# Windowed attention and a gated MLP on one core: all four first scores ahead of the first product, another order of decoding, and a stored 1e-9

## The chip, the core and the metric

The kernel runs on one core of a Trainium2 chip. A core has a matrix engine (TensorE, PE; its weight loads are shown as PEld), VectorE (DVE), ScalarE (ACT), GpSimd (POOL) and SyncE (SP), which issues the transfers; each runs its own queue of instructions in order. Work is held in SBUF (128 partitions), products in PSUM. The metric is device time in microseconds (us); lower is better.

## The reference

```python
scores = scale * np.matmul(q, k.transpose(0, 1, 3, 2))        # 8 batches, 8 heads, 576 positions, 64 wide
scores = np.where(masks[None, :, :, :], scores, -1000000000.0)  # heads 0-3: last 32; heads 4-7: 32 at a step of 4
scores = scores - np.max(scores, axis=-1, keepdims=True)
attn = np.exp(scores)
attn = attn / (np.sum(attn, axis=-1, keepdims=True) + 1e-09)
x = np.matmul(attn, v)               # then (8 * 576 tokens, 512 values)
h = x @ w_in                         # 512 -> 2048
g = h * (1.0 / (1.0 + np.exp(-1.702 * h)))
return g @ w_out                     # 2048 -> 512
```

All inputs are float32.

## The kernel before

**Attention** goes by *pairs*: two heads of one batch, so pair k = 4b + c is batch b, heads 2c and 2c+1 (c = 2, 3 are the dilated ones). The first four pairs (k < 4) belong to batch 0, and the MLP can start only on their result. For such a pair `scores` (lines 470 and 482) writes the mask into the PSUM bank `sp` by a product with the identity and adds q·k in small tiles; `exponentials` takes the maximum (L502), subtracts it into the probabilities `pr` (L349) and takes the exponential on ScalarE (L506). Then come the sum over 64 keys (L520), the addition of 1e-9 (L510) and the reciprocal (L512) into `sm`, the multiplication of `pr` by it in two halves (GpSimd or VectorE, L349), two transposes into `ct` (L529), and `first_product` (L575) into `first_x`. `drain_x` splits that result into a high and a low part, `xs` (ScalarE copies, L342; VectorE subtracts, L349). There are two sets of `pr`, `sm` and `ct`, used in turn, a third one for later pairs, and one bank pair `sp`. Before, pair k + 1's score and pair k's product stand one behind the other, and each drain after its product.

**Decoding.** The weights come as 64-bit floats. `decode(n)` loads one column block of `w_in` or one row block of `w_out` (128 of the 2048 hidden values each), and makes a float32 value of it in eight steps: L394 and L395 (ScalarE), the sign (L388 on ScalarE or L390 on VectorE), L398 (VectorE), an addition (L349), a high part (L342 or L344) and a low part (L349). Before, n counts w_in 0, w_out 0, w_in 1, w_out 1 and so on.

**The MLP.** For batches 0 to 2, column block f is `hps[f]` (L848: 4 parts of x, 3 matmuls each of 512 columns), then tanh (L856), gate (L857) and split into `gh` and `gl`, then 12 matmuls into four accumulators (L785 to L789). The other batches use sums and differences of blocks, so that 7 products do the work of 8 (lines 991 and 1106).

**The order** isn't written out. `Plan.add` notes every operation with a cost for each engine that may do it, an urgency, and the names it reads and writes; `Plan.placed` runs a list schedule over these costs and so fixes each engine's queue before anything is built. It also models that PE fetches its instructions in blocks of 256 (`fetched`), and fills PE's planned gaps up to 60 us with matmuls into `idle` (L1237 of 512 columns; L1241 small ones, which only move PE on to the next block of instructions). A changed cost or urgency can so change the order anywhere.

## Time and profile before

| what | value |
|---|---|
| time, median of 3 runs (lowest to highest) | 829.03 us (828.74 to 829.33) |
| profiled execution: time, span | 828.89 us, 827.2 us |
| busy: PE, DVE, ACT, POOL | 98%, 81%, 62%, 40% of the span |
| mean granted TensorE clock | 0.991 |
| moved over the span | 188.12 MB, mean 227 GB/s |

A row of an engine in order of time has start, length, engine, line, operation, written and read tile, count, and in brackets the idle time before it and what ended it. Lengths in the profile are in us unless ns is written.

### The profile page before, as it was taken

The numbers are of one execution on the slowest core, as the hardware profiler recorded it, in microseconds if no ns is written. First come the engines' busy times: TensorE is split into PE (matmuls) and PEld (weight loads), VectorE is DVE, ScalarE is ACT, GpSimd is POOL, SyncE is SP. The second block draws the span as 40 slices with busy tenths as digits, with TensorE's granted clock in tenths as the row PEclk, the third lists the DMA queues.
The fourth block names the chain that finished last, engine by engine and source line by source line (L and its number), as shares of the span: only waits on it lengthen the run. The fifth ranks groups of instructions, "written<-read, shape, count | busy, mean of one in ns | idle before, by whom it ended". The sixth has DMA issues, their size and how long they took to land.

```text
span 827.2 us, 18837 instructions
## 1 busy us (share of the span) xinstructions
PE 811.2 (98%) x7240; PEld 653.5 (79%) x7240; DVE 669.7 (81%) x1104; ACT 515.0 (62%) x992; POOL 327.8 (40%) x296
## 2 busy tenths in 40 slices
PE   7899999999999999999999999999999999999997
PEld 4678777888878888878788788888888888888886
DVE  6898989787888778898989998977679876867575
ACT  7998986676676777586776655446446544544340
POOL 3343336566655663324235357331125431112251
PEclk8799999999999999999999999999999999999999
DMA  9476658889757567868878878675665658664546
GB/s 359 152 244 193 181 192 287 295 281 314 249 189 254 183 200 257 267 190 280 279 229 261 261 233 260 219 269 168 214 193 182 211 186 273 203 222 149 189 151 181
DMA packets 109610, 188.12 MB, mean 227 GB/s; under 512 B 26448, under 2 KB 55376, under 8 KB 109520
## 3 DMA queue, kind: packets, MB, share of 16 engines
q1 hardware_dynamic: 109376, 186.78, 69.3%
q8 instruction: 57, 0.93, 0.5%
q14 instruction: 33, 0.27, 0.1%
q10 hardware_dynamic: 144, 0.13, 0.0%
HBM read 140.64 MB, written 45.09 MB: 225 GB/s over the span
## 4 chain that ended last, share of the span: by engine, by line
PE 88%; DVE 7%; ACT 1%; issue 1%; DMA 1%; SPq 0%; DVEq 0%; ACTq 0%
PE hp_m L848 15%; PE up_q L991 9%; PE up_r L991 9%; PE up_p L991 8%; PE second_q_Q L1106 5%; PE second_r_Q L1106 5%; PE second_p_Q L1106 5%; PE acc_m L785 5%; PE acc_m L789 5%; PE acc_m L786 4%; PE sp L482 3%; PE second_r_Z L1106 3%; PE second_R L1106 3%; PE second_q_Z L1106 3%; PE second_p_Z L1106 2%; PE av L607 2%
## 5 line engine op out<-in xcount | busy, mean ns | idle before, releaser
L349 POOL TENSOR_TENSOR arena<-arena 128x256 f32<-128x256 f32 (+3 forms) x109 | 118.0, 1091 | 155.7 <-DVE wi_last_units L349 34.7
L848 PE MATMUL hp_m<-xs,wi_kept 128*128 128x512 f32 x504 | 129.1, 398 | 0.7 <-DVE xs L349 0.4
L848 PEld LDWEIGHTS hp_m<-xs,wi_kept 128*128 128x128 f32 x504 | 93.3, 188 | 22.5 <-DVE arena L857 1.6
L342 ACT ACTIVATE wo_kept<-arena 128x512 fp32r<-128x512 f32 x115 | 71.9, 629 | 42.3 <-PE second_r_Q L1106 11.4
L349 POOL TENSOR_TENSOR wo_kept<-arena,wo_kept 128x512 fp32r<-128x512 f32 x34 | 45.3, 1340 | 105.5 <-ACT wo_kept L342 72.2
L991 PE MATMUL up_p<-wi_kept,xs 128*128 128x512 f32 x336 | 84.7, 394 | 2.2 <-DVE arena L349 1.3
L991 PE MATMUL up_r<-wi_kept,xs 128*128 128x512 f32 x336 | 85.3, 389 | 0.0
L991 PE MATMUL up_q<-wi_kept,xs 128*128 128x512 f32 x336 | 83.4, 389 | 0.0
L991 PEld LDWEIGHTS up_p<-wi_kept,xs 128*128 128x128 f32 x336 | 62.1, 188 | 16.8 <-DVE arena L349 2.2
L991 PEld LDWEIGHTS up_q<-wi_kept,xs 128*128 128x128 f32 x336 | 63.0, 188 | 13.4 <-DVE arena L1013 0.3
L991 PEld LDWEIGHTS up_r<-wi_kept,xs 128*128 128x128 f32 x336 | 63.1, 188 | 13.1
L349 DVE TENSOR_TENSOR wo_kept<-arena,wo_kept 128x512 fp32r<-128x512 f32 x87 | 65.3, 761 | 5.9 <-ACT wo_kept L342 5.4
L349 POOL TENSOR_TENSOR wo_kept<-wi_last_units,wo_kept 128x512 fp32r<-128x512 f32 x23 | 31.9, 1388 | 84.6 <-ACT wo_kept L342 84.6
L785 PE MATMUL acc_m<-gh,wo_kept 128*128 128x512 f32 x156 | 61.7, 395 | 0.4 <-ACT arena L342 0.3
L786 PE MATMUL acc_m<-gh,wo_kept 128*128 128x512 f32 x156 | 60.9, 390 | 0.0
L349 POOL TENSOR_TENSOR pr<-pr,sm 128x320 f32<-128x320 f32 x52 | 43.3, 850 | 43.0 <-DVE sm L512 29.3
L342 ACT ACTIVATE bt<-ct 32x256 f32<-32x256 f32 (+1 forms) x127 | 55.2, 435 | 3.2 <-DVE ct L533 0.9
L1012 ACT ACTIVATE arena<-arena 128x512 f32<-128x512 f32 x60 | 37.5, 628 | 28.9 <-DVE arena L349 25.1
L349 DVE TENSOR_TENSOR gl<-arena,gh 128x512 fp32r<-128x512 f32 x53 | 44.9, 847 | 9.1 <-PE acc_m L789 6.4
L349 DVE TENSOR_TENSOR arena<-arena 128x512 f32<-128x512 f32 (+1 forms) x68 | 50.4, 747 | 0.4
L1013 DVE SCALAR_TENSOR_TENSOR arena<-arena 128x512 f32<-128x512 f32 x60 | 48.1, 807 | 0.7 <-ACT arena L1012 0.2
L342 ACT ACTIVATE wo_kept<-wi_last_units 128x512 fp32r<-128x512 f32 x47 | 29.6, 629 | 30.0 <-PE second_r_Z L1106 8.9
(261 smaller groups left out, 1826.6 us busy)
## 6 DMA issues: line engine op xcount, KB each, us to landing
xs<-sums SPq DMA_DIRECT2D x168, 256.0 KB, 3.3
out_weights<-sums_o SPq DMA_DIRECT2D x63, 512.0 KB, 3.8
qk<-qk_dram SPq DMA_DIRECT2D x29, 576.0 KB, 5.2
xs<-sums_o SPq DMA_DIRECT2D x21, 512.0 KB, 3.6
v<-vp_dram SPq DMA_DIRECT2D x28, 320.0 KB, 4.4
sums<-arena SPq DMA_DIRECT2D x32, 256.0 KB, 3.6
sums_o<-arena SPq DMA_DIRECT2D x32, 256.0 KB, 3.4
arena<-wi_dram SPq DMA_DIRECT2D x15, 512.0 KB, 4.7
```

Of the source, the lines that this page charges most:

```text
L342: A.activation(dst, src, AF.Copy, scale=scale)
L349: (V if e == DVE else G).tensor_tensor(out=dst, in0=a, in1=b, op=op)
L482: T.matmul(dst[:, w:w + n], u["qk"][rows, at:at + 32], u["qk"][rows, S + first:S + first + n], start=not masked(k), stop=True, tile_positi ...
L607: T.matmul(u["x"][i][rows, at:at + last - first], u["v"][keys, a, m], bt[keys, m, a, first:last], start=(bank_, a) not in begun, stop=True ...
L785: T.matmul(self.acc[j], w[:, 0, cols], high, start=f == 0, stop=False)
L786: T.matmul(self.acc[j], w[:, 1, cols], high, start=False, stop=False)
L789: T.matmul(self.acc[j], w[:, 0, P * j:P * j + P], low, start=False, stop=f == NF - 1)
L848: T.matmul(hps[f], wi(f)[:, st, cols], mv[:, c], start=c == 0 and k == 0, stop=c == NC - 1 and k == 2)
L991: T.matmul(self.banks[place], xs[:, slot, at:at + P], wi_kept[:, 2 * a + c, mv], start=fresh and c == 0 and k == 0, stop=c == 1 and k == 2 ...
L1012: add({ACT: 0.60}, -10.0, lambda e: A.activation(unit(tmp), src(), AF.Tanh, scale=0.851), need, own(tmp))
L1013: add({DVE: -0.70 if need[0][0] == "A" else 0.70}, -10.0, lambda e: V.scalar_tensor_tensor(out=unit(dst), in0=unit(tmp), scalar=1.0, in1=s ...
L1106: T.matmul(self.second[key], w[:, st, cols], mv, start=fresh and y == 0 and k == 0, stop=y == 1 and k == 2, skip_group_check=True)
```

## The change

1. `first_attention` is split. It now adds the loads, the scores and the softmax of each of the four pairs. `first_transposed` (the two transposes of a pair) is added behind the softmax for pairs 0 and 1, and for pairs 2 and 3 behind the products of pairs 0 and 1. `first_multiplied` (product and drain) reads the key `scores3`, so that no product stands ahead of the fourth score.
2. The set of probabilities gets a 65th column, which holds 1e-9; the sum runs over 65 values, and the addition of 1e-9 goes. Two VectorE memsets write that column for two sets at the start, and one memset for the third set before the third batch. `pr` is a view of the first 64.
3. Decoding takes w_in 0, w_in 1, w_out 0, w_in 2, then the others in the old order.
4. The memset of `bt` has urgency 44 instead of 20; the model of a fetched block takes 4.2 instead of 6.1 before 6 us.

```diff
-                blocks.append(at + (6.1 if at < 18.0 else 4.2))
+                blocks.append(at + (4.2 if at < 6.0 else 6.1 if at < 18.0 else 4.2))
...
-    prs = [fixed([P, 2, QT, W], F32, f"pr{j}") for j in range(2)]
+    sets = [fixed([P, 2, QT, W + 1], F32, f"pr{j}") for j in range(2)]
...
-    prs.append(third[:, 0:2 * QT * W].rearrange("p (a t w) -> p a t w", a=2, t=QT))
+    sets.append(third[:, 0:2 * QT * (W + 1)].rearrange("p (a t w) -> p a t w", a=2, t=QT))
+    prs = [p[:, :, :, 0:W] for p in sets]
...
+    for p in sets[0:2]:
+        V.memset(p[:, :, :, W], 1.0e-9)
...
+    order = [(0, 0), (0, 1), (1, 0), (0, 2)]
+    order += [(i % 2, i // 2) for i in range(2 * NF) if (i % 2, i // 2) not in order]
...
-        add({DVE: -0.15}, urgency, lambda e: V.tensor_scalar(
-            out=sm, in0=sm, scalar1=1.0e-9, scalar2=None, op0=ALU.add), (), (SM,))
...
-        add({DVE: 0.80}, urgency, lambda e: V.tensor_reduce(out=sm, in_=pr, axis=AX.X, op=ALU.add), (PR,), (SM,))
+        add({DVE: 0.81}, urgency, lambda e: V.tensor_reduce(out=sm, in_=sets[y], axis=AX.X, op=ALU.add), (PR,), (SM,))
...
-    def first_attention(k, urgency):
+    def first_attention(k):
         load_qk(k)
         load_v(k)
-        add({PE: 1.5 if k else 2.3}, urgency - 1.0e5, lambda e: scores(k), (lots(k)[0],), ("sp",), count=180)
-        softmax(k, urgency)
-        add({PE: 1.4}, urgency - 1.0e5, lambda e: first_product(k), (lots(k)[1], f"ct{turn(k)}.0", f"ct{turn(k)}.1"), FOUR,
-            count=184)
-        drain_x(k, urgency)
+        add({PE: 1.5 if k else 2.3}, k - 1.0e5, lambda e: scores(k), (lots(k)[0],), ("sp", f"scores{k}"), count=180)
+        softmax(k, k)
+    def first_transposed(k):
+        y = turn(k)
+        pr, ct = prs[y], cts[y].rearrange("p h t a q -> p (h t a q)").rearrange("p (a t w) -> p a t w", a=2, w=W)
+        for a in range(2):
+            add({DVE: 0.48}, k, lambda e, a=a: V.transpose(out=ct[:, a, 0:QT], in_=pr[:, a]), (f"pr{y}", f"pr{y}.{a}"), (f"ct{y}.{a}",))
+    def first_multiplied(k):
+        y = turn(k)
+        add({PE: 1.4}, k - 1.0e5, lambda e: first_product(k), (lots(k)[1], f"ct{y}.0", f"ct{y}.1", f"scores{NC - 1}"),
+            FOUR, count=184)
+        drain_x(k, k)
...
     for c in range(NC):
-        first_attention(c, c)
+        first_attention(c)
+        if c < 2:
+            first_transposed(c)
         if c in (1, 2):
             decode(c - 1, c + 1.3)
+    for c in range(NC):
+        first_multiplied(c)
+        if c < 2:
+            first_transposed(c + 2)
...
-            add({POOL: 1.2}, 20.0, lambda e: G.memset(bt, 0.0), (), ("bt", "btl", *zeroed))
+            add({POOL: 1.2}, 44.0, lambda e: G.memset(bt, 0.0), (), ("bt", "btl", *zeroed))
```

What stands in the queues now, at three places. Line numbers grow by about 20 in the changed kernel: L482 is L490 there, L575 is L576, L349 is L353, L342 is L346, L388 is L396, L394 and L395 are L402 and L403.

PE, from the third score on, before (`sp_320` and `sp_439` are the third and fourth score; `ct_91` and `ct_92` the transposed probabilities of the pairs in turn):

```order
L482 MATMUL sp_320<-arena 32x64 x3
L482 MATMUL sp_320<-arena 32x48
L482 MATMUL sp_320<-arena 32x16
L575 MATMUL first_x<-ct_91,v_129 64x32 x6
L575 MATMUL first_x<-ct_91,v_129 64x64 x24
L575 MATMUL first_x<-ct_91,v_129 64x48 x8
L575 MATMUL first_x<-ct_91,v_129 64x16 x8
```

and in the changed kernel, where `sp_405` is the fourth score:

```order
L490 MATMUL sp_405<-arena 32x64 x3
L490 MATMUL sp_405<-arena 32x48
L490 MATMUL sp_405<-arena 32x16
L576 MATMUL first_x<-ct_91,v_131 64x32 x6
L576 MATMUL first_x<-ct_91,v_131 64x64 x24
L576 MATMUL first_x<-ct_91,v_131 64x48 x8
L576 MATMUL first_x<-ct_91,v_131 64x16 x8
```

The first product moved from behind the third score to behind the fourth. Of fillers, there stand now 19 small and 2 large ones behind the first score (before: 7 large), 6 behind the second (9), 10 behind the third (none before the first product), 6 behind the first product (3), 1 ahead of the third and 6 ahead of the fourth product. Between the second and the fourth product stand 12 matmuls of the first two column blocks, and behind the fourth product 15 that don't need its result.

DVE, from the fourth pair's maximum on, before:

```order
L502 TENSOR_REDUCE mx_86<-sp_439 128x10
L529 STREAM_TRANSPOSE ct_91<-pr_83 128x320
L349 TENSOR_TENSOR pr_84<-sp_439,mx_86 128x640
L529 STREAM_TRANSPOSE ct_91<-pr_83 128x320
L349 ISA arena<-bt,arena 128x1024
L520 TENSOR_REDUCE sm_89<-pr_84 128x10
L349 TENSOR_TENSOR xs<-first_x,xs 128x432
L349 TENSOR_TENSOR xs<-first_x,xs 128x80
L510 TENSOR_SCALAR sm_89<-sm_89 128x10
L512 RECIPROCAL sm_89<-sm_89 128x10
```

and in the changed kernel:

```order
L510 TENSOR_REDUCE mx_86<-sp_405 128x10
L353 TENSOR_TENSOR pr_84<-sp_405,mx_86 128x10x64
L695 STREAM_TRANSPOSE ct_91<-pr_83 128x320
L353 TENSOR_TENSOR xs<-first_x,xs 128x432
L353 TENSOR_TENSOR xs<-first_x,xs 128x80
L695 STREAM_TRANSPOSE ct_91<-pr_83 128x320
L526 TENSOR_REDUCE sm_89<-pr_84 128x10
L518 RECIPROCAL sm_89<-sm_89 128x10
```

The drain that stands here (`xs<-first_x`) was the second pair's and is now the first pair's; the addition of 1e-9 (L510 before) is gone, and the long addition of the decoding went to GpSimd.

ACT, from the third pair's drain to the fourth's, before:

```order
L342 ACTIVATE xs<-first_x 128x4x128
L394 ACTIVATE arena<-arena 128x512 x2
L395 ACTIVATE arena<-arena 128x512 x2
L388 ACTIVATE arena<-arena 128x512
L342 ACTIVATE xs<-first_x 128x4x128
```

and in the changed kernel:

```order
L346 ACTIVATE xs<-first_x 128x4x128
L346 ACTIVATE wi_kept<-arena 128x512
L403 ACTIVATE arena<-arena 128x512
L396 ACTIVATE arena<-arena 128x512
L346 ACTIVATE wo_kept<-arena 128x512
L346 ACTIVATE xs<-first_x 128x4x128
```

Two high parts (`wi_kept`, `wo_kept`) now stand between the two drains instead of three steps of decoding.

More of the change, by code (lines that the diff above doesn't have):

```diff
@@ L290, in tile_windowed_attention_then_gated_mlp @@
     third = area(13, 3)
-    prs.append(third[:, 0:2 * QT * W].rearrange("p (a t w) -> p a t w", a=2, t=QT))
-    cts.append(third[:, 2 * QT * W:4 * QT * W].rearrange("p (h t a q) -> p h t a q", h=2, a=2, t=QT))
+    sets.append(third[:, 0:2 * QT * (W + 1)].rearrange("p (a t w) -> p a t w", a=2, t=QT))
+    prs = [p[:, :, :, 0:W] for p in sets]
+    cts.append(third[:, 2 * QT * (W + 1):2 * QT * (2 * W + 1)].rearrange("p (h t a q) -> p h t a q", h=2, a=2, t=QT))
     four = tc.tile_pool(name="four", bufs=1, space=bass.MemoryType.PSUM)
@@ L353, in tile_windowed_attention_then_gated_mlp @@
     words = arena[:, 6:9].bitcast(U32)
+    order = [(0, 0), (0, 1), (1, 0), (0, 2)]
+    order += [(i % 2, i // 2) for i in range(2 * NF) if (i % 2, i // 2) not in order]
     def decode(n, urgency):
-        f = n // 2
-        if n % 2:
+        out_, f = order[n]
+        if out_:
             src, hi, lo, key = w_out[f], wo(f)[:, 0], wo(f)[:, 1], f"wo{f}"
@@ L525, in softmax @@
         if k < NC:
-            for a in range(2):
-                to = ct.rearrange("p h t a q -> p (h t a q)")[:, a * QT * W:a * QT * W + QT * W]
-                add({DVE: 0.48}, urgency, lambda e, a=a, to=to: V.transpose(
-                    out=to, in_=pr[:, a].rearrange("p t w -> p (t w)")), (PR, f"{PR}.{a}"), (f"{CT}.{a}",))
             return
@@ L706, in attention @@
             if k == FIRST * NC:
+                add({DVE: 0.10, POOL: 0.10}, urgency, lambda e: (V if e == DVE else G).memset(sets[2][:, :, :, W], 1.0e-9),
+                    (), ("pr2", "first v3", "first qk3"))
                 for j in range(k + 1, n):
@@ L751, in unit @@
             if n < 6:
-                return prs[n - 4].rearrange("p a t w -> p (a t w)")[:, 0:GT]
+                return sets[n - 4].rearrange("p a t w -> p (a t w)")[:, 0:GT]
             return cts[n - 6].rearrange("p h t a q -> p (h t a q)")[:, 0:GT]
```

## The prediction

> **What bounds the kernel now.** I read the page first, then the busy time by stage, then the first 45 us engine by engine in order of time.
>
> ```profile
> span 827.2 us, 18837 instructions
> PE 811.2 (98%) x7240; PEld 653.5 (79%) x7240; DVE 669.7 (81%) x1104; ACT 515.0 (62%) x992; POOL 327.8 (40%) x296
> 10.00:20.00 10.00, 7.87 (x276) 4.62 (x256) 7.57 (x18) 8.67 (x13) 5.48 (x6) 0.81 1.03 411
> 20.00:30.00 10.00, 7.50 (x223) 5.00 (x223) 9.46 (x20) 9.26 (x15) 5.37 (x6) 0.50 0.55 190
> 30.00:40.00 10.00, 9.57 (x177) 6.72 (x161) 7.76 (x17) 8.94 (x13) 2.79 (x3) 1.00 0.33 102
> 40.00:60.00 20.00, 20.00 (x226) 15.86 (x225) 19.29 (x34) 18.40 (x31) 7.75 (x7) 1.00 0.77 257
> 300.00:500.00 200.00, 197.75 (x1796) 159.79 (x1795) 175.23 (x286) 136.02 (x291) 76.41 (x66) 1.00 0.78 251
> ```
>
> (In the stage rows: stage, its length, then busy time of PE, PEld, DVE, ACT, POOL, then granted clock, DMA share, GB/s.) From 40 us on PE has no gap worth a name; the largest stage loss is 2.25 us of 200. Up to 40 us PE is "busy" too, but largely with filler: the matmuls into `idle`, whose result nobody reads, and small attention products. There VectorE and ScalarE are at 76 to 95%, and from 20 to 30 us the granted clock is 0.50. So the time is a constant amount of matrix work plus the moment from which PE does it without a pause. The change can gain only by moving that moment. This is how PE comes to it:
>
> ```profile
> 4.22 0.69 PE L470 MATMUL sp<-plain,ident 128*128 128x320 bf16 x2 [1.64 <-DVE plain L328]
> 5.07 1.44 PE L482 MATMUL sp<-qk 64*32 64x64 f32 x84 [0.15 <-DMA qk<-qk_dram]
> 6.44 3.14 PE L1237 MATMUL idle<-ident 128*128 128x512 bf16 x7
> 10.79 2.12 PE L1237 MATMUL idle<-ident 128*128 128x512 bf16 x9
> 13.42 0.84 PE L482 MATMUL sp<-arena 64*32 64x64 f32 x63
> 16.02 0.40 PE L482 MATMUL sp<-arena 64*32 64x64 f32 x21 [1.76 <-issue]
> 16.35 1.66 PE L575 MATMUL first_x<-ct,v 32*64 32x32 f32 x92
> 22.31 1.37 PE L482 MATMUL sp<-arena 64*32 64x64 f32 x75 [1.60 <-issue]
> 23.61 1.18 PE L575 MATMUL first_x<-ct,arena 32*64 32x32 f32 x53
> 25.70 0.91 PE L575 MATMUL first_x<-ct,arena 32*64 32x64 f32 x39 [0.90 <-issue]
> 29.42 1.23 PE L575 MATMUL first_x<-ct,arena 32*64 32x64 f32 x80
> 34.00 1.08 PE L575 MATMUL first_x<-ct,arena 32*64 32x64 f32 x80
> 38.18 3.92 PE L848 MATMUL hp_m<-xs,wi_kept 128*128 128x512 f32 x16 [0.43 <-DVE xs L349]
> 0.00:38.10 38.10, 6.83 (x20) 3.88 (x20) 0.82 0.66 249
> 61.29 2.72 PE hp_m L848 x12
> ```
>
> The last two rows are line 848 alone before 38.1 us (20 matmuls), and the length of 12 at full clock, 2.72/12 = 0.227 us each. The score product of the third pair stops for 1.76 us, that of the fourth for 1.60, the second pair's product for 0.90, each put down to "issue". Between the last two stops lie 75 + 53 = 128 matmuls, each with its weight load: 256 PE instructions. So PE stops where a block of 256 instructions is not there yet, and the stops' ends lie 22.31 - 16.02 = 6.29 and 25.70 - 22.31 = 3.39 us apart. Without pause PE runs from 38.18 on, with 20 useful matmuls done. I carry both into one figure, the **base**: 38.18 - 20 x 0.227 = 33.64 us, as if PE had started from nothing there. The gain is the base before less the base after, less what PE then waits anew.
>
> **The change, part by part.** *Fourth score before the first product.* The score bank is free when VectorE has subtracted the maximum.
>
> ```profile
> 12.09 0.82 DVE L349 TENSOR_TENSOR pr<-sp,mx 128x640 f32<-128x640 f32 x1
> 24.46 0.50 DVE L529 STREAM_TRANSPOSE ct<-pr 128x320 f32<-128x320 f32 x1
> 27.45 0.76 DVE L349 TENSOR_TENSOR xs<-first_x,xs 128x432 fp32r<-128x432 f32 x2
> 28.12 1.20 DVE L510 TENSOR_SCALAR sm<-sm 128x10 f32<-128x10 f32 x1
> 37.04 1.09 DVE L349 TENSOR_TENSOR xs<-first_x,xs 128x512 fp32r<-128x512 f32 x1
> L510 DVE TENSOR_SCALAR sm<-sm x32: 113/169/1196, 11.2 to 445.9; 128x10 f32<-128x10 f32 x32
> 25.76 0.74 ACT L506 ACTIVATE pr<-pr 128x640 f32<-128x640 f32 x1 [0.29 <-DVE pr L349]
> 27.29 0.64 ACT L342 ACTIVATE wi_kept<-arena 128x512 fp32r<-128x512 f32 x1
> 28.33 1.36 ACT L388 ACTIVATE arena<-arena 128x512 f16<-128x512 f32 x1
> 32.65 1.24 ACT L395 ACTIVATE arena<-arena 128x512 uint32<-128x512 uint32 x2
> 35.11 1.09 ACT L342 ACTIVATE xs<-first_x 128x512 fp32r<-128x512 f32 x1
> 6.00:35.10 29.10, 24.46 (x681) 15.28 (x662) 23.22 (x48) 25.85 (x37) 12.22 (x13) 0.77 0.69 266
> 26.72 0.90 POOL L1207 MEMSET bt<- 128x960 f32 x1 [1.54 <-DVE arena L349]
> 29.65 1.73 POOL L349 TENSOR_TENSOR pr<-pr,sm 128x320 f32<-128x320 f32 x2 [0.36 <-DVE sm L512]
> L533 DVE STREAM_TRANSPOSE ct<-pr 128x320 f32<-128x320 f32 x44 | 20.5, 491 | 0.5 <-POOL pr L349 0.5
> arena<-wi_dram SPq DMA_DIRECT2D x15, 512.0 KB, 4.7
> ```
>
> The 19 small filler matmuls behind the first score are 76 PE instructions, so the block boundary that lay in the second score now lies at about 7 us. The block behind it is asked for some 3 us sooner, and the third score's stop of 1.76 us should go. The next boundary still falls in the fourth score, which now comes one product earlier: third score at about 13, crossing at 13.4, plus 6.3 for a block, gives 19.7 and an end of the fourth score, call it S, at 19.9. That is the early bound. The late one comes from the clock. After the first score now stand two large filler matmuls instead of seven. Seven took 3.14 (0.45 each), nine took 2.12 a little later (0.235 each): the clock doubled in between. If the thinner filler does not raise it, six fillers cost 2.7 instead of 1.4 and the ten behind the third score up to 4.5 instead of 2.35. Then the fourth score ends at about 21.5. Before it ended at 22.31 + 1.37 = 23.68, so S moves up by 2.2 to 3.8 us. The Trainium skill, "Runtime: NRT & Kernel Launch", section "Instruction fetch mechanics", holds that crossing a block of 256 instructions is mostly hidden. By that there would be no stops, and S would be near 19.2; the rows above, with 1.76, 1.60 and 0.90, disagree.
>
> *The chain from S to the last drain.* In the new order each product waits for the drain of the one before (its last VectorE subtraction). From S: maximum and subtraction (0.82 each), one transpose 0.50, the drain's two subtractions 0.76, together 2.9: second product. It takes 1.25; ScalarE meanwhile has an exponential 0.74, a high part 0.64, two L395 (1.24) and a copy (about 0.2) ahead of the drain, so the drain (about 0.7) starts at S + 4.9, and with 0.76 on VectorE the third product starts at S + 6.3. The third drain has two L388 of 1.36, one shorter step and a copy ahead of it on ScalarE, starts at S + 8.7, takes 1.09 and 1.04: fourth product at S + 10.8, end at S + 12.0 when filler and first matmuls run at full clock. With S = 21.5 that is 33.5. With S = 19.9 the two stops of the fourth score let the clock drop as it did at 16 us, and six fillers, six matmuls and one filler at about 0.45 sit between the products: about 34.1. As early bound I take ScalarE alone: it was busy 25.85 of the 29.10 us up to the last drain at 35.11, and its queue to that drain loses an L388, an L394 and an L395 and gains two high parts and a copy, net 1.36 + 2 x 0.62 - 2 x 0.64 - 0.2 = 1.1 (L394 taken like L395). So that drain cannot start before 35.11 - 3.25 - 1.1 = 30.8. I take 33.5, because ScalarE has work queued at each link and the late S brings the full clock.
>
> At that end 12 matmuls of line 848 are done, and 15 more stand ahead of the first that needs the fourth drain: 3.4 us, against 2.3 to 3.3 for the drain. So PE runs without a gap from there: base 33.5 - 12 x 0.227 = 30.8, gain 33.64 - 30.8 = 2.8. The bounds give 31.4 (gain 2.2) and 30.7 - 2.7 = 28.0 (gain 5.6).
>
> *Given back.* Behind the last drain the fourth column block needs weights that were decoded at leisure before. VectorE and ScalarE were at 96% and 92% from 40 to 60 us, so a PE that is three us earlier meets them: tanh, gate and split behind an L388 (1.36) leave PE idle for 0 to 1.1 us at the fourth column block. I take 0.4. From 60 us on the cover is PE itself.
>
> *The 1e-9.* 32 VectorE instructions go, 8 us in sum by the L510 row's mean of about 0.25; four lie in the start, the one at 28.12 held for 1.20 beside POOL's work. What they free there is in the chain already (none stands in it). Later PE hides them: were it not so, at most the 2.25 us of its gaps in 300 to 500 would be won. The sums read 650 instead of 640 values (0.01 us each). The two small memsets stand ahead of the identity matrix and so of the mask: the first mask product would end 0.1 to 0.2 later than 4.91, against operands that land at 5.07, so 0 to 0.1. Rows are now 65 apart; nothing in the trace prices this for exponentials and products. From below it is 0; from above a tenth of them, 0.3 per pair, 1.2 us in the start. I take 0, because the transposes of later groups (L533) read rows that aren't packed and take 0.49, like the 0.50 of L529.
>
> *Zeros put off* (0.90 on POOL at 26.72): it stood ahead of the multiplications at 29.65; it now follows them. *Decoding order*: as many transfers of the same size in the same places; only which weights come first differs, so that two column blocks are ready when the first drain is. It adds a load of the fourth weight after the second product, at about 26, and ScalarE comes to it at about 32: 6 us against 4.7 to landing.
>
> **Sum.** The profiled execution took 828.89 (span 827.2 and 1.7 around it), 0.14 under the median 829.03. 828.89 - 2.8 + 0.4 = 826.5; against the median 826.6. I say 826.5.
>
> **The rivals.** *Slower, through the clock.* If the two fillers leave the clock at half from 9 us to the end of the fourth product, the fixed number of fillers becomes a burden: third score's mask at 13.9, ten fillers until 20.4, S at 22.6, products at 24.3, 28.5, 33.1 and 39.9 (1.66 each, six fillers 2.6, six matmuls 2.6). Base 37.2, 3.5 later: 832.4. It decides from an end of the fourth product at 36.4. For it: 20 to 30 us at 0.50 before, with as much filler. Against it: ten fillers in a row last longer than the seven that raised the clock at 9.5. The Trainium skill, "TensorE: Matmul & The Clock Gate", section "Part 1: The HAM clock gate (the "warmup" mystery)", lets the full clock come after about 3.4 us of activity; by it the ten fillers would raise it and this rival falls. 10%.
>
> *Decoding paces the start.* PE comes early, but VectorE at 96% gives the weights no sooner, and the 2.4 us come back as waits between 36 and 60: 828.9, no change. For it: the 96 and 92%; against it: POOL is busy 7.75 of these 20 us and can take split work. 20%.
>
> *All of it is won.* S at 19.9 and a clock that stays up: fourth product ends at 32.0, base 29.2, gain 4.4 and 0.4 back: 824.9. 20%.
>
> *The rows of 65 cost a fifth on ScalarE and POOL,* or the changed order opens gaps later: 1 to 2 us lost against the forecast, 828; 5%.
>
> **How the numbers follow.** Forecast 45%, own range 825.5 to 827.5. A measurement here tells 0.2%, 1.66 us, from none. Faster: all of the full gain (20), nine tenths of the forecast (41), a little of the rest: 0.62. Within 0.2%: the rest of the forecast, the pacing, the dear rows: 0.25. Slower: the clock rival and a little of the pacing, 0.13. The range 824.0 to 830.0 leaves out the clock rival and a tail of the full gain.
>
> **What would show it.** The stop in the third score gone and one left in the fourth; its end between 19.9 and 21.5; products one after another, the fourth ending near 33.5; a first matmul run without gap from there; the L1228 memset behind the fourth pair's multiplications. Wrong would be: a clock of 0.50 past 27 us, PE gaps of over 1.5 us in all between 36 and 60, or later stages that differ by more than a microsecond.

## The result, and the profile after

The changed kernel takes 824.28 us (median; 822.45 to 825.62) against 829.33 (828.74 to 829.45) for the kernel before: the ratio is 0.9941, with a 95% interval of 0.9927 to 0.9954. It is 5.05 us faster; 826.5 was forecast, within 824.0 to 830.0, and 825.5 to 827.5 as the forecast's own range, which the result misses. The profiled execution took 822.45 us, the lowest of the changed kernel's times, so its profile shows 6.4 us of gain (828.89 - 822.45), 1.8 us better than the median. Where sizes matter below, a second profile of the same order that lies nearer to the median stands beside it.

The page's first rows and the busy time by stage, after (stage, its length, busy PE, PEld, DVE, ACT, POOL, granted clock, DMA share, GB/s):

```profile
span 820.7 us, 18890 instructions
PE 809.3 (99%) x7279; PEld 653.4 (80%) x7279; DVE 669.0 (82%) x1081; ACT 518.0 (63%) x988; POOL 328.4 (40%) x294
10.00:20.00 10.00, 8.42 (x229) 4.58 (x216) 8.28 (x17) 9.05 (x13) 6.14 (x7) 1.00 1.02 410
20.00:30.00 10.00, 9.71 (x301) 6.77 (x302) 7.78 (x16) 8.32 (x16) 6.36 (x8) 0.83 0.61 208
40.00:60.00 20.00, 20.00 (x226) 15.81 (x224) 19.64 (x34) 19.25 (x31) 8.46 (x7) 1.00 0.75 260
300.00:500.00 200.00, 199.82 (x1805) 161.59 (x1804) 175.09 (x277) 135.92 (x283) 89.86 (x72) 1.00 0.78 253
```

From 20 to 30 us the clock is 0.83 where it was 0.50, and PE is busy 9.71 of 10 us where it was 7.50. And, which no term of the prediction held, the stage from 300 to 500 us has lost its gaps: 0.18 us are left of 2.25.

PE in order of time, after:

```profile
10.76 2.74 PE L1258 MATMUL idle<-ident 128*128 128x512 bf16 x6
13.97 1.13 PE L490 MATMUL sp<-arena 64*32 64x64 f32 x84
15.03 2.33 PE L1258 MATMUL idle<-ident 128*128 128x512 bf16 x10
17.56 0.86 PE L490 MATMUL sp<-arena 64*32 64x64 f32 x65
20.25 0.37 PE L490 MATMUL sp<-arena 64*32 64x64 f32 x19 [1.83 <-issue]
20.55 1.49 PE L576 MATMUL first_x<-ct,v 32*64 32x32 f32 x92
21.96 2.63 PE L1258 MATMUL idle<-ident 128*128 128x512 bf16 x6
24.53 1.16 PE L576 MATMUL first_x<-ct,arena 32*64 32x32 f32 x92
27.43 1.42 PE L576 MATMUL first_x<-ct,arena 32*64 32x64 f32 x80
31.68 1.08 PE L576 MATMUL first_x<-ct,arena 32*64 32x64 f32 x80
32.69 7.11 PE L863 MATMUL hp_m<-xs,wi_kept 128*128 128x512 f32 x27
39.63 0.39 PE L800 MATMUL acc_m<-gh,wo_kept 128*128 128x512 f32 x1
```

The third score runs through. One stop is left, in the fourth score, which ends at 20.62. The stretch behind it runs at half clock: six fillers in 2.63 us, where ten behind the third score took 2.33. The six behind the second score were as slow (2.74 us), although the clock column shows 1.00 from 10 to 20 us; the slow pace up to about 13.5 us has to be read from the lengths. The fourth product ends at 32.76, and 27 matmuls of the first layer follow in one row.

Other engines in the same stretch, after (VectorE, ScalarE and GpSimd in order of time):

```profile
9.48 0.83 DVE L526 TENSOR_REDUCE sm<-pr 128x10 f32<-128x650 f32 x1 [0.20 <-ACT pr L514]
22.09 0.66 ACT L346 ACTIVATE xs<-first_x 128x432 fp32r<-128x432 f32 x2 [1.07 <-PE first_x L576]
25.74 0.66 ACT L346 ACTIVATE xs<-first_x 128x432 fp32r<-128x432 f32 x2 [0.61 <-PE first_x L576]
28.34 0.90 POOL L1228 MEMSET bt<- 128x960 f32 x1
```

ScalarE waited for the first two products, 1.07 and 0.61 us, rather than they for it. The sum over 650 values takes 0.83.

The rest of the way is read at three points that both kernels pass: the first matmul into the accumulators, the first into `up_p` and the first into `up_q` (the block of sums). Matmuls of these lines, each row with their count, the smallest, median and largest ns of one, and the first and the last start in us; before:

```profile
L785 PE MATMUL acc_m<-gh,wo_kept x156: 387/389/504, 41.9 to 333.7; 128*128 128x512 f32 x156
L991 PE MATMUL up_p<-wi_kept,xs x336: 387/389/500, 342.5 to 483.6; 128*128 128x512 f32 x168
L991 PE MATMUL up_q<-wi_kept,xs x336: 389/389/501, 486.6 to 633.5; 128*128 128x512 f32 x168
```

and after:

```profile
L800 PE MATMUL acc_m<-gh,wo_kept x156: 387/389/504, 39.6 to 330.6; 128*128 128x512 f32 x156
L1006 PE MATMUL up_p<-wi_kept,xs x336: 387/389/501, 337.9 to 477.2; 128*128 128x512 f32 x168
L1006 PE MATMUL up_q<-wi_kept,xs x336: 388/389/498, 480.2 to 627.5; 128*128 128x512 f32 x168
```

At the first accumulation the changed kernel is 41.9 - 39.6 = 2.3 us ahead and has done 39 matmuls of the first layer instead of 36, 3 x 0.227 = 0.7 us more: a lead of 3.0 us. At `up_p` it is 4.6, at `up_q` 6.4, at the end 6.5 (827.2 - 820.7). So 3.0 us come from the start, where they were looked for, and 3.5 from later on, nearly all of it by 486 us, where nothing was expected. PE's waits from there on, before, and then after (in sum, how often, the longest):

```profile
PE up_p L991 <- DVE arena L349: 1.3, 2, 0.7
PE up_p L991 <- DVE arena L1013: 0.9, 1, 0.9
```

```profile
PE hp_m L863 <- DVE arena L872: 0.9, 1, 0.9
PE up_p L1006 <- DVE arena L353: 0.2, 1, 0.2
```

2.2 us of waits in the block of sums became 0.2.

### The profile page after: what moved, and what is told of

It is laid out like the page before. It is cut to its first block, busy times and chain, and to the rows that moved or that the text cites. A ratio compares the mean times of both kernels' runs of the same rounds, so it can differ in the third digit from the quotient of the medians.

```text
span 820.7 us, 18890 instructions
## 1 busy us (share of the span) xinstructions
PE 809.3 (99%) x7279; PEld 653.4 (80%) x7279; DVE 669.0 (82%) x1081; ACT 518.0 (63%) x988; POOL 328.4 (40%) x294
## 4 chain that ended last, share of the span: by engine, by line
PE 97%; DMA 1%; DVE 1%; issue 0%; ACT 0%; SPq 0%; DVEq 0%
PE hp_m L863 16%; PE up_p L1006 10%; PE up_r L1006 9%; PE up_q L1006 9%; PE acc_m L800 5%; PE second_p_Q L1121 5%; PE second_q_Q L1121 5%; PE acc_m L804 5%; PE acc_m L801 5%; PE second_r_Q L1121 5%; PE sp L490 4%; PE second_q_Z L1121 3%; PE second_r_Z L1121 3%; PE second_R L1121 3%; PE second_p_Z L1121 3%; PE av L608 2%
## 5 line engine op out<-in xcount | busy, mean ns | idle before, releaser
L353 POOL TENSOR_TENSOR arena<-arena 128x256 f32<-128x256 f32 (+3 forms) x94 | 100.7, 1083 | 97.8 <-DVE wi_last_units L353 21.6
L353 POOL TENSOR_TENSOR wo_kept<-arena,wo_kept 128x512 fp32r<-128x512 f32 x41 | 56.9, 1395 | 131.5 <-ACT wo_kept L346 84.9
L346 ACT ACTIVATE wo_kept<-arena 128x512 fp32r<-128x512 f32 x111 | 69.2, 630 | 40.7 <-PE second_r_Q L1121 10.9
L353 DVE TENSOR_TENSOR wo_kept<-arena,wo_kept 128x512 fp32r<-128x512 f32 x80 | 61.1, 775 | 5.1 <-ACT wo_kept L346 4.7
L346 ACT ACTIVATE bt<-ct 32x256 f32<-32x256 f32 (+1 forms) x130 | 56.6, 435 | 11.7 <-DVE ct L534 6.0
L353 POOL TENSOR_TENSOR pr<-pr,sm 128x320 f32<-128x320 f32 x52 | 43.7, 856 | 48.5 <-DVE sm L518 43.5
L800 PE MATMUL acc_m<-gh,wo_kept 128*128 128x512 f32 x156 | 61.5, 394 | 0.0
L353 POOL TENSOR_TENSOR wo_kept<-wi_last_units,wo_kept 128x512 fp32r<-128x512 f32 x22 | 29.9, 1361 | 78.3 <-ACT wo_kept L346 72.3
L353 DVE TENSOR_TENSOR arena<-arena 128x512 f32<-128x512 f32 (+1 forms) x75 | 59.1, 797 | 2.7 <-ACT arena L346 1.8
L801 PE MATMUL acc_m<-gh,wo_kept 128*128 128x512 f32 x156 | 60.8, 390 | 0.0
L1028 DVE SCALAR_TENSOR_TENSOR arena<-arena 128x512 f32<-128x512 f32 x60 | 49.8, 837 | 1.7 <-ACT arena L1027 1.3
L346 ACT ACTIVATE gh<-arena 128x512 fp32r<-128x512 f32 x57 | 36.0, 631 | 17.5 <-DVE arena L872 5.8
L353 DVE TENSOR_TENSOR gl<-arena,gh 128x512 fp32r<-128x512 f32 x53 | 41.3, 779 | 6.5 <-ACT gh L346 3.2
```

Of the source, the lines that this page charges most:

```text
L346: A.activation(dst, src, AF.Copy, scale=scale)
L353: (V if e == DVE else G).tensor_tensor(out=dst, in0=a, in1=b, op=op)
L800: T.matmul(self.acc[j], w[:, 0, cols], high, start=f == 0, stop=False)
L801: T.matmul(self.acc[j], w[:, 1, cols], high, start=False, stop=False)
L1028: add({DVE: -0.70 if need[0][0] == "A" else 0.70}, -10.0, lambda e: V.scalar_tensor_tensor(out=unit(dst), in0=unit(tmp), scalar=1.0, in1=s ...
```

## The experiments

"Lead" below is always worked out as above from one profiled execution: at the first accumulation (41.9 less its start, plus 0.227 us for each matmul of the first layer beyond 36), and at the end of the span (827.2 less it).

**Two kernels for the 1e-9.** In the changed kernel VectorE adds 1e-9 again ahead of each reciprocal, inside the same planned operation, so that no queue is otherwise changed (it is then counted twice, which adds 1e-9 more to each sum). In the kernel before, the addition is left out, and with it the 1e-9.

```diff
-        add({DVE: 0.19}, urgency, lambda e: V.reciprocal(out=sm, in_=sm), (), (SM,))
+        def work(e):
+            V.tensor_scalar(out=sm, in0=sm, scalar1=1.0e-9, scalar2=None, op0=ALU.add)
+            V.reciprocal(out=sm, in_=sm)
+        add({DVE: 0.19}, urgency, work, (), (SM,))
```

```diff
-        add({DVE: -0.15}, urgency, lambda e: V.tensor_scalar(
-            out=sm, in0=sm, scalar1=1.0e-9, scalar2=None, op0=ALU.add), (), (SM,))
+        add({DVE: -0.15}, urgency, lambda e: None, (), (SM,))
```

> The changed kernel with its queues in the same order, and the addition of 1e-9 put back directly ahead of each of the 32 reciprocals (the 65th column stays, so 2e-9 is added in all). The lead over the kernel before is 3.0 us at the first accumulation and 6.4 at the end in the profiles (medians: 5.05). Theory A (the removed additions relieve VectorE later on and make the part after the start): a good part of the later 2 to 3 us goes, 825.5 to 827. Theory B (the part after the start comes from the order that was planned anew): 824.3 to 824.8, at most 0.5 more than the changed kernel. Theory C (the start alone counts and the rest is chance between runs): 824.3 as well, with the same spread.

> The kernel before with its queues in the same order, and only the 32 additions of 1e-9 left out (the sum is used without them). Theory A: 826 to 828, with the waits at 363 to 370 us smaller. Theory B and C: 828.6 to 829.3; in the start, PE waits for blocks of its program, not for VectorE, so the 1.2 us held at 28 us give at most 0.5.

Measured: 824.32 us with the additions put back, ratio to the kernel before 0.9942 to 0.9969, against 0.9927 to 0.9954 without them; and 829.86 us for the kernel before without them, 0.9999 to 1.0016. The 32 additions are worth nothing that can be measured, in either order, and theory A falls: without them the kernel before still waits 1.3 and 0.9 us at `up_p`. The first of these runs serves as the second profile of the changed order, at 824.00 us: first accumulation at 40.0 with 39 matmuls done, end of the span 822.3. Its lead is 2.6 in the start and 4.9 at the end. Its queues are those of the changed kernel, and yet its one stop in the fourth score is shorter (0.91 us, until 20.10) and the clock stays at 1.00 from 20 to 30 us. The fourth score ends at 20.47, the six fillers take 1.47 us, and the second product starts at 23.42:

```profile
23.42 0.32 PE L580 MATMUL first_x<-ct,arena 32*64 32x32 f32 x10 [0.45 <-ACT pr L514]
```

**The order of the products alone.** The kernel before with all four scores ahead of the first product and the transposes placed as in the change, and nothing else (the diff in part):

```diff
-        add({PE: 1.4}, urgency - 1.0e5, lambda e: first_product(k), (lots(k)[1], f"ct{turn(k)}.0", f"ct{turn(k)}.1"), FOUR,
-            count=184)
-        drain_x(k, urgency)
...
+    for c in range(NC):
+        first_multiplied(c)
+        if c < 2:
+            first_transposed(c + 2)
```

> The kernel before with one part alone: all four first scores ahead of the first product and the transposes placed as in the change; old decoding order, old 1e-9, old model of the blocks, so no small fillers behind the first score. Theory P (the order of the products is what moves the start): 825.5 to 827. Theory F (the arrival of PE's program blocks is what moves it, and the order only matters with it): the third score stops again at about 14.3 until 16.0, the fourth score is cut by a block that comes at about 22.3, the end of the scores is near 23, and the time is 828 to 829.5.

Measured: 829.44 us, 0.9994 to 1.0014: no change. PE in order of time:

```profile
16.33 0.53 PE L482 MATMUL sp<-arena 64*32 64x64 f32 x21 [1.79 <-issue]
22.80 1.06 PE L570 MATMUL first_x<-ct,v 32*64 32x64 f32 x79 [1.10 <-issue]
33.54 1.08 PE L570 MATMUL first_x<-ct,arena 32*64 32x64 f32 x80 [0.61 <-DVE xs L349]
41.76 0.50 PE L792 MATMUL acc_m<-gh,wo_kept 128*128 128x512 f32 x1 [0.84 <-ACT gh L342]
```

The fourth product starts at 33.54, 0.46 sooner than before. In the old order of decoding PE then waits 0.84 at the accumulation for ScalarE's split. Lead at the first accumulation: 0.1 us. The third score's stop and the time are those of theory F; the next stop came in the first product, though, not in the fourth score.

**The fetch model alone.** The kernel before with the 4.2 before 6 us.

```diff
-                blocks.append(at + (6.1 if at < 18.0 else 4.2))
+                blocks.append(at + (4.2 if at < 6.0 else 6.1 if at < 18.0 else 4.2))
```

> The kernel before with one part alone: the model takes 4.2 us for a block asked for before 6 us, which puts 19 small fillers and 2 large ones behind the first score in place of 7 large ones. Theory F: the third score's stop of 1.76 us goes, the first product comes 1.5 to 2 us sooner, the next stop moves on; 827 to 828. Theory P: the stop goes, but nothing is won, since the products still alternate with the scores: 828.6 to 829.5. The slower rival of the prediction (the thinner filler leaves the clock at half) would give 830 or more.

Measured: 829.85 us, 1.0004 to 1.0023: no gain, if anything 0.1% lost, near theory P. PE in order of time:

```profile
15.16 1.07 PE L482 MATMUL sp<-arena 64*32 64x64 f32 x84
16.70 0.99 PE L575 MATMUL first_x<-ct,v 32*64 32x32 f32 x71
21.55 0.62 PE L575 MATMUL first_x<-ct,v 32*64 32x48 f32 x21 [3.86 <-issue]
```

The third score is whole, as in the changed kernel. But the next boundary then falls into the first product, and PE stops there for 3.86 us, longer than both stops of the scores before together (1.76 + 1.60). In this execution (833.41 us, the slowest of its twelve) the first accumulation starts at 42.6 with 42 matmuls done, a lead of 0.7.

**The change with the old order of the products.**

```diff
-        add({PE: 1.4}, k - 1.0e5, lambda e: first_product(k), (lots(k)[1], f"ct{y}.0", f"ct{y}.1", f"scores{NC - 1}"),
+        add({PE: 1.4}, k - 1.0e5, lambda e: first_product(k), (lots(k)[1], f"ct{y}.0", f"ct{y}.1"),
...
         first_attention(c)
-        if c < 2:
-            first_transposed(c)
+        first_transposed(c)
+        first_multiplied(c)
...
-    for c in range(NC):
-        first_multiplied(c)
-        if c < 2:
-            first_transposed(c + 2)
```

> The changed kernel with one part undone: the first products alternate with the scores again (with the new decoding order, the stored 1e-9 and the small fillers kept). So far no part alone has moved the time. Theory P+F (the order of the products and the early blocks are needed together): the start falls back, a stop of about 3.9 us lands in the first product as it did with the small fillers alone, and the time is 827 to 829. Theory D (the new decoding order is what moves the start): 824 to 825.5.

Measured: 831.92 us, 1.0019 to 1.0043, 0.3% slower than the kernel before and outside the ranges of both theories. PE in order of time:

```profile
20.40 0.44 PE L576 MATMUL first_x<-ct,v 32*64 32x16 f32 x16 [3.76 <-issue]
33.44 1.08 PE L576 MATMUL first_x<-ct,arena 32*64 32x64 f32 x80
```

The same stop of almost four microseconds in the first product, and yet the lead at the first accumulation (41.7, 39 matmuls done) is 0.9. What makes it slower lies behind: its span is 831.2, so 4.9 us are lost between the first accumulation and the end.

**The change with the old fetch model,** so without the small fillers, planned anew.

```diff
-                blocks.append(at + (4.2 if at < 6.0 else 6.1 if at < 18.0 else 4.2))
+                blocks.append(at + (6.1 if at < 18.0 else 4.2))
```

> The changed kernel with one part undone: the model takes 6.1 us for every block before 18 us, so seven large fillers and no small ones stand behind the first score. Theory P+F: the third score stops at about 14.3 for 1.8 us again and the products come as they did with their order alone, the fourth ending at about 34.6 instead of 32.8; 826 to 827.5. Theory D: the stop returns, but the time stays at 824 to 825.5.

Measured: 832.11 us, 1.0022 to 1.0052, 7.8 us more than the changed kernel and again outside both theories. The third score stops again, for 0.77 us. But at the first accumulation (41.2, 39 done) only 1.6 of them are there. PE's waits from 36 us on, the first row:

```profile
PE second_p_R L1121 <- DMA out_weights<-sums_o: 2.1, 1, 2.1
```

From `up_p` to `up_q` it needs 148.3 us where the changed kernel needs 142.3. One number in a model of the first 6 us gives a different order at 400 us.

**The same again with the order held fixed.** To part the two, the changed kernel's order is kept and only the 19 small fillers aren't issued (nothing but filler is left out).

```diff
             n = misc["small"] = misc.get("small", 0) + 1
+            if n > 49:
+                return
```

> The changed kernel with every queue in the same order, only the 19 small fillers behind the first score are not issued (76 PE instructions fewer, nothing planned anew). Theory F (blocks of PE's program): the boundary goes back into the second score, the third score stops again for 1 to 2 us near 14 to 16, the fourth score or the first product is cut later, the fourth product ends 1 to 2 us after 32.8, and the time is 825.5 to 827. If the blocks don't matter and the order does it all: 824.0 to 824.6.

Measured: 824.44 us, 0.9931 to 0.9955, the same as the changed kernel, as if the order did it all. PE in order of time:

```profile
16.11 0.35 PE L490 MATMUL sp<-arena 64*32 64x48 f32 x13 [0.62 <-issue]
22.30 1.01 PE L576 MATMUL first_x<-ct,v 32*64 32x64 f32 x73 [1.93 <-issue]
32.47 1.08 PE L576 MATMUL first_x<-ct,arena 32*64 32x64 f32 x80
```

and its stage from 20 to 30 us:

```profile
20.00:30.00 10.00, 7.55 (x279) 5.48 (x280) 8.13 (x19) 8.36 (x16) 6.12 (x7) 1.00 0.56 203
```

The stop in the third score is back at 0.62 us and the other has moved into the first product (1.93 for 1.83). The fourth product starts 0.8 later, and the median shows nothing of it. So the small fillers move a stop, and are worth no more than a few tenths; the 7.8 us of the run above are the price of another order.

**Another later order.** The planner has a constant, ROOM, by which it multiplies an operation's cost when it works out how late that operation may come; these due times count from 130 us on. With 3.1 or 2.9 for 3.0 the queues up to the first accumulation stay nearly as they are, and those behind change. Four kernels: the changed one and the one before, each with both values.

```diff
-ROUNDS, SINCE, CALM, ROOM = 3, 130.0, 8.0, 3.0
+ROUNDS, SINCE, CALM, ROOM = 3, 130.0, 8.0, 3.1
```

> The changed kernel with the plan's ROOM at 3.1 instead of 3.0, a constant that weighs only what is placed past 130 us: the same start, another order later on. Theory B (the 2 to 3 us won behind the start hang on the order that came out of the plan): the first accumulation at 39.6 as in the changed kernel, and a time that differs from 824.3 by 0.5 to 2 either way. If the later part follows from the earlier start itself: 824.0 to 824.6.

> The kernel before with ROOM at 3.1: the same start as before, another order past 130 us. Theory B: up to 2 us off 829.3 either way, with the waits of the first sums of blocks at 363 to 370 us changed or gone. If the later part follows from the start: 829.0 to 829.6 with those waits as they were.

> The changed kernel with ROOM at 2.9, a third order past 130 us behind the same start. With ROOM 3.0 and 3.1 it took 824.3 and 827.1. Theory B (the later order is chance, the start is worth about 3): anywhere from 823 to 829, and 2 to 5 less than the kernel before with ROOM 2.9. If the change brings a better later order of itself: below 826, and 4 or more below the kernel before with the same constant.

> The kernel before with ROOM at 2.9: with 3.0 and 3.1 it took 829.3 to 829.7 and 831.4. Theory B: anywhere from 828 to 833; the mean of the three differences between the two kernels with the same constant is then the worth of the start, near 3 us.

Measured, the median and the ratio to the kernel before as it was:

| ROOM | kernel before | changed kernel | changed less before |
|---|---|---|---|
| 3.0 | 829.33 us | 824.28 us (0.9927 to 0.9954) | -5.05 |
| 3.1 | 831.36 us (1.0006 to 1.0029) | 827.10 us (0.9958 to 0.9979) | -4.26 |
| 2.9 | 829.68 us (1.0003 to 1.0020) | 827.30 us (0.9973 to 0.9996) | -2.38 |

The start of the changed kernel is nearly the same in all three (lead 3.0, 2.4 and 2.2 at the first accumulation), and yet the time differs by 3 us, more than the 0.5 to 2 us that was expected of 3.1. A row from PE's waits with 3.1:

```profile
PE second_p_Q L1121 <- DMA out_weights<-sums_o: 1.7, 1, 1.7
```

This wait stands in no row of the changed kernel. So a part of the 5.05 us hangs on the later order that 3.0 happened to give; in all three pairs the change is still faster, by 3.9 us in the mean (near 3 was expected).

**Fewer fillers behind the first product.** The order is held, and four of the six large fillers there aren't issued (nothing but filler is left out). It tests the clock, and whether fillers hold up the second product.

```diff
+                m = misc["large"] = misc.get("large", 0) + 1
+                if 21 <= m <= 24:
+                    return
                 T.matmul(misc["idle"], ident, ident[:, None, :].broadcast_to([P, GT // P, P]), start=True, stop=True)
```

> The changed kernel with every queue in the same order, only four of the six large fillers behind the first product are not issued. In the profile of the changed kernel they hold the second product until 24.53, while the drain it waits for ended at 23.66. If each product really hangs on the drain before it, the second product starts near 23.8 and the rest moves up by 0.5 to 0.8: 823.5 to 823.8. If ScalarE paces the drains: no change, 824.0 to 824.6. If the clock then stays at half for another stretch of 3.4 us: 825 or more.

Measured: 825.21 us, 0.9946 to 0.9970. Stages of this kernel, and then of the changed one (columns as above):

```profile
24.00:27.00 3.00, 2.23 (x94) 1.88 (x94) 2.71 (x7) 2.68 (x7) 0.47 (x1) 0.50 0.38 150
27.00:30.00 3.00, 3.00 (x7) 1.66 (x6) 2.28 (x5) 3.00 (x6) 2.94 (x4) 0.50 0.56 175
```

```profile
24.00:27.00 3.00, 3.00 (x100) 2.11 (x98) 2.86 (x6) 2.39 (x7) 1.82 (x3) 0.94 0.45 122
27.00:30.00 3.00, 2.96 (x88) 2.27 (x87) 1.75 (x6) 3.00 (x4) 2.53 (x4) 1.00 0.45 162
```

PE in order of time, with fewer fillers:

```profile
25.11 1.65 PE L576 MATMUL first_x<-ct,arena 32*64 32x32 f32 x92 [0.77 <-ACT pr L514]
26.69 2.93 PE L863 MATMUL hp_m<-xs,wi_kept 128*128 128x512 f32 x6
34.29 1.08 PE L576 MATMUL first_x<-ct,arena 32*64 32x64 f32 x80
```

The drain that the second product waits for, its last step:

```profile
24.25 0.76 DVE L353 TENSOR_TENSOR xs<-first_x,xs 128x432 fp32r<-128x432 f32 x2 [0.26 <-ACT arena L346]
```

The fourth score ends later here, at 21.30 + 0.50 = 21.80. Counted from there (S), the second product is sooner: S + 3.3 instead of S + 3.9. The row names an exponential as what it waited for, but that had ended at 24.85; the drain ended at 24.25 + 0.76 = 25.01, 0.1 us ahead of the product. So the product hangs on the drain, and the fillers did hold it in the changed kernel. What outweighs this is the clock: it stays at half beyond 30 us (it is 0.78 from 30 to 33, so until about 31.3), and six useful matmuls take 2.93 us instead of 1.65.

The fourth product starts at 34.29 instead of 31.68. Of these 2.6 us, 1.2 are the later S: the fourth score came 0.4 later and its stop took 2.48 us for 1.83. Both lie ahead of the fillers that were left out; in five executions of this start that stop took 0.91 to 2.48 us. The first accumulation starts at 42.3 with 39 matmuls done, a lead of 0.3. The median is 0.9 above the changed kernel's, and the two intervals overlap.

**The parts of the lead, side by side.** Each row is one profiled execution. The first four rows have the changed kernel's later order, and the last one has that of the kernel before.

| kernel | time of this execution | lead at the first accumulation | lead at the end | gained (+) or lost between |
|---|---|---|---|---|
| changed | 822.45 | 3.0 | 6.5 | +3.5 |
| changed, additions back | 824.00 | 2.6 | 4.9 | +2.3 |
| changed, small fillers not issued | 823.13 | 2.1 | 5.8 | +3.7 |
| changed, four fillers not issued | 826.33 | 0.3 | 2.6 | +2.3 |
| changed, ROOM 3.1 | 828.14 | 2.4 | 0.8 | -1.6 |
| changed, ROOM 2.9 | 829.69 | 2.2 | -0.7 | -2.9 |
| changed, old fetch model | 832.02 | 1.4 | -3.1 | -4.5 |
| changed, old order of products | 833.32 | 0.9 | -4.0 | -4.9 |
| before, products behind the scores | 827.62 | 0.1 | 1.3 | +1.2 |
| before, new fetch model | 833.41 | 0.7 | -4.6 | -5.3 |
| before, ROOM 3.1 | 830.36 | 0.0 | -1.4 | -1.4 |
| before, ROOM 2.9 | 829.33 | -0.2 | -0.4 | -0.2 |
| before, additions left out | 830.20 | -1.4 | -1.3 | +0.1 |

The four executions of the same later order all gain 2.3 to 3.7 us behind the first accumulation, whatever their start was. The order of the kernel before repeats as well: without the additions it is within 0.1 of the kernel before behind the first accumulation, though that execution had lost 1.4 in the start. The eight other orders lie between -5.3 and +1.2. So the later part is a property of the plan, not of the execution, and it is the other half of the gain. The start varies more from one execution to the next: 2.2 to 3.0 in four of the changed start (changed, additions back, both ROOM), -1.4 to 0.0 in four of the old one. In the mean they lie 2.95 us apart.

## Why the prediction was right, and where it wasn't

**Right by its steps in the start.** The stop in the third score is gone and one is left in the fourth. That score ends at 20.62, within 19.9 to 21.5. The products follow one another from S + 3.9 (forecast S + 2.9), S + 6.8 (S + 6.3) and S + 11.1 (S + 10.8); the end of the fourth at S + 12.1 (S + 12.0). S came earlier than the 21.5 that was taken, because the ten fillers behind the third score ran at full clock (2.33 us, where up to 4.5 was allowed for). So the end is 32.76 instead of 33.5, the first matmuls run from there without a gap, and the base is 32.76 - 12 x 0.227 = 30.04 instead of 30.8. The second link was a microsecond late because six fillers stood ahead of it at half clock until 24.59, while the drain had ended at 22.90 + 0.76 = 23.66. In the second profile of this order, where those fillers ran at full clock, it started at 23.42, which is S + 2.95, as forecast. The drain in the changed kernel:

```profile
22.90 0.76 DVE L353 TENSOR_TENSOR xs<-first_x,xs 128x432 fp32r<-128x432 f32 x2
```

The next two links made up for a part of it, since ScalarE was free when the second product ended. The gain in the base is 3.6 (2.8 forecast). Given back: the 27 matmuls would have handed on at 32.76 + 27 x 0.227 = 38.89, and the accumulation started at 39.63, 0.74 later. Before, the same sum, 38.18 + 16 x 0.227 = 41.81 against 41.94, gives 0.13; so 0.6 are given back where 0.4 was taken. PE's own rows hardly show it, but its weight loads do:

```profile
38.53 0.19 PEld L863 LDWEIGHTS hp_m<-xs,wi_kept 128*128 128x128 f32 x1 [0.54 <-ACT wi_kept L346]
39.07 0.30 PEld L863 LDWEIGHTS hp_m<-xs,wi_kept 128*128 128x128 f32 x2 [0.35 <-DVE wi_kept L353]
```

This is the fourth column block, the place that was forecast. Its first load starts just after a gate on VectorE (L872) has ended at 38.42; the high part of its weights, which the row names, had ended at 38.21. The second load waits for the low part of the weights, which ended at 39.01. The net 3.0 stands against 2.4 forecast; in the execution near the median it is 2.6. The 1e-9 is worth nothing, and the rows of 65 cost nothing (0.83 for the sum, 0.50 for a transpose, both as before). The memset of `bt` came behind the fourth pair's multiplications, as foreseen. Putting its urgency back to 20 gives the same queues on every engine, so that part does nothing by itself.

**The step that failed** is the one that priced everything later at nothing: "From 60 us on the cover is PE itself." The sign named for it, later stages that differ by more than a microsecond, is there twice in this profile: 1.6 us from the first accumulation to `up_p`, 1.8 from there to `up_q`. PE does cover what the other engines do, but the list schedule is made anew from the first changed cost on, and which drain comes a little too late for PE at 365 us is then dealt out again. The term that was left out is 2.3 to 3.7 us in the executions of this order, about 2 us by the medians (5.05 less the 2.6 to 3.0 of the start). Its sign could not have been forecast from the trace of before: seven of the other eight orders lost, by 0.2 to 5.3 us. That 2.2 us of waits stood at `up_p` before could have been read, and they were, in sum, as "at most 2.25 us would be won", but only for the 1e-9. Of the 1.6 us between 42 and 342 us, 0.5 is work put off: the changed kernel reaches `up_p` with 58 of the accumulation's matmuls on `wo_last` (L800, L801) done, the kernel before with 60. For the other 1.1 PE's waits show nothing (0.8 us idle in sum before, 1.0 after); their cause stays open. The prediction's survey also passed over the last stage: from 700 us to the end PE is idle for 5.1 us before and 4.8 after, so that this end plays no part in the gain.

**Luck.** The start alone, 3.0 us at best, would have given about 826, near the forecast. That the gain is about twice the forecast one, and the time still 0.28 us inside the range, is chance: with the two other values of ROOM the same start gave 827.10 and 827.30.

**What the parts do.** None of the three tried alone lowers the time: the order of products alone gives 829.44, the fetch model alone 829.85, the additions left out 829.86. (Each of the first two has a later order of its own; their leads in the start are 0.1 and 0.7.) In the changed order, the additions and the small fillers can be taken back at no loss that shows. What is left is the order of the products with the order of decoding: the first without the second has a lead of 0.1 in the start, the second without the first 0.9, both 2.1 to 3.0 in the changed start, 1.4 with the old fetch model planned anew, and 0.3 with four fillers left out. This goes by exclusion: the order of decoding alone, in the kernel before, was not run, and the changed kernel with only its decoding put back has no time, since in that plan the queues wait for one another and none can go on. So what the order of decoding is worth by itself is not shown.

**The rivals.** *Slower, through the clock,* fell: the ten fillers behind the third score took 2.33 us, full clock, and the 0.83 from 20 to 30 us stands for 3.4 us at half clock. The mechanism is real, though: without four fillers the clock was 0.50 up to 30 us, and the lead of the start fell to 0.3, though 1.2 us of that fall is the later S. That the clock comes back as the second product starts fits the Trainium skill, "TensorE: Matmul & The Clock Gate", section "Part 1: The HAM clock gate (the "warmup" mystery)", which lets the full clock come after one busy window of about 3.4 us: in the changed kernel PE was busy without a gap from 20.25 on, and the clock was full again at about 24.4 (0.94 from 24 to 27 us). With four fillers fewer PE was busy without a gap from 25.11 on, and the full clock came only at about 31.3, 6.2 us later; one such window doesn't give that delay, and its cause stays open. *Decoding paces the start* fell: VectorE is at 98% and ScalarE at 96% from 40 to 60 us, and PE has no gap there; what it gave back, 0.6 us, lies just ahead, at 38 to 39 us. *All of it is won* named 824.9, which is close to the result, but for another reason: S was not 19.9, and the start gave 3.0, not 4.0. *Gaps later* was the right kind of event with the wrong sign.

On the blocks of instructions the Trainium skill, "Runtime: NRT & Kernel Launch", section "Instruction fetch mechanics", has the crossing mostly hidden. Here it isn't: 1.83 us in the changed kernel, and 3.86 and 3.76 where the boundary lay in the first product.

## What to carry to other kernels

Where a planner sets the order, a change in the first microseconds deals out the whole order again: give that a term of its own, of a few microseconds and either sign, and measure it by moving a constant that should not matter, in both kernels. To price one part of a change, hold the order and leave out the instructions; the small fillers cost 7.8 us when their model was taken back and the plan made anew, and nothing when the order was held. A lead is best read at points that both kernels pass, so that what the start gave isn't mixed with what came later.

## What was unexpected of the hardware

A block of 256 PE instructions came about six microseconds after PE had crossed into the block ahead of it: 5.95 us in the changed kernel (crossed at about 14.3 by the count of instructions, next block at 20.25), 6.29 before. That isn't a constant: the block after it took 3.39 us in the kernel before (22.31 to 25.70). Filler ahead of a boundary moved the cut to another instruction; a cut in the first product cost 0.69 to 3.86 us, one in a score 0.62 to 2.49.

A stop doesn't always lower the clock: with the small fillers not issued, PE stopped for 0.62 and 1.93 us and the clock was 1.00 from 20 to 30 us; with a single stop of 1.83 it fell to half, and with 0.91 in the same queue it stayed at 1.00. What decides is not shown. And one profile is read with an error of a microsecond or two: the changed kernel's six times lie between 822.45 and 825.62, and 29 later ones of the kernel before between 827.85 and 831.76.
